# Two parts of a matmul operand moved by 64 and 240 bytes inside their SBUF slot

## The chip, the cores and the metric

The kernel runs on one core of a Trainium2 chip. The metric is device time in microseconds, the median of three runs. All PE (TensorE) work, all vector work on DVE (VectorE), ACT (ScalarE) and POOL (GpSimd), and the transfers issued by SP (SyncE) belong to that one core.

## What is computed

The reference filters each sequence in the frequency domain and then runs a gated feed-forward layer on every token.

```python
def _attn_ref(x, w_r, w_i, b_r, b_i):          # x: 8 x 3008 x 256
    X = np.fft.rfft(x, axis=1)
    Yr = Xr @ w_r - Xi @ w_i + b_r
    Yi = Xr @ w_i + Xi @ w_r + b_i
    # soft threshold by 0.01 on both
    y = np.fft.irfft(Y, n=x.shape[1], axis=1)
def _moe_ref(x, w_in, w_out):                  # x: 24064 x 256, 256 -> 2048 -> 256
    h = x @ w_in
    relu6 = np.clip(h + 3.0, 0.0, 6.0)
    g = h * relu6 / 6.0
    return (g @ w_out).astype(np.float32)
```

## The kernel before

The transform is done as small matmuls (47 by 64 points) with transfers through DRAM between the stages. Those stages are cut into pieces and put between the pieces of the feed-forward layer by a written-out list of slots (`slots`, `fill`).

The feed-forward layer works on 47 blocks of 512 tokens (`c`) and 8 pieces of 256 hidden channels (`f`), which gives 376 units (`units`). Each full-precision matrix product is made of three fp32r products: every operand is split into a high part (the value rounded to fp32r) and a low part (the rest), and low times high, high times low and high times high are added in PSUM.

One unit `i` goes through these steps, which run over four passes of the main loop:

- The input product is done with seven block products of 256 columns (a Strassen scheme; tiles `yb` against `w_in`, into PSUM tiles `pb` and `ps_a`). Each block product is three matmuls: 21 matmuls of 256 columns. ACT and DVE collect them into the tile `h`.
- `gate(i)`: ACT makes `r` from `h` (L1099), DVE makes r = min(r, 6) * h (L1101). ACT then writes the high part of `r` into the tile `gs` in two halves of 512 columns (L1104), and DVE writes the low part, `r` minus high, in one instruction of 1024 columns (L1105).
- `down(i, u, dh)`: four groups, one for each half `u` of the hidden channels and each half `dh` of the output. Each group is three matmuls of 512 columns in this order: `w_out_lo` with high `gs`, `w_out_hi` with high `gs`, `w_out_hi` with low `gs`. That is 12 matmuls of 512 columns for a unit, all through the helper line L137, where `gs` is the moving operand (its columns stream through the array) and `w_out` is the loaded weight. The low part is read by one in three of them: 4 for a unit, 1504 in all.

`gs` has two buffers. A buffer is one slot of 4 * 512 + 64 = 2112 floats for each partition, 64 more than the two parts need; the same slots hold tiles of the first transform (`xin`, `a`, `X`) before the first unit. In the built program both slots start at a multiple of 64 bytes (byte 115840 and byte 124288 of the partition), and so do the buffers of `yb`, of `w_in` and of `w_out`. The order on PE is fixed: what `group`, `phase_1`, `phase_2`, `phase_b` to `phase_e` and `fill` emit stands in program order.

Of the kernel before, what the change touches and what calls it, by code (L numbers as in the profile page):

```python
# [9 lines left out]
F32 = mybir.dt.float32  # L10
F32R = mybir.dt.float32r
# [3 lines left out]
ALU = mybir.AluOpType  # L15
# [6 lines left out]
B, S, D, FF = 8, 3008, 256, 2048  # L22
# [3 lines left out]
P = 128  # L26
# [6 lines left out]
T = 512  # L33
# [68 lines left out]
def spectral_ffn(ctx: ExitStack, tc: tile.TileContext, x, w_r, w_i, bias, w_in, w_out, f47, f64, g64, g64u, sgn, out):  # L102
    nc = tc.nc
# [10 lines left out]
    def space(shape, dt, name, tag=None):  # L114
        tag = tag or name
        return sb.tile(shape, dt, name=name, tag=tag, bufs=depth.get(tag, 1))
# [11 lines left out]
    def split(hi, lo, src, on=None):  # L128

        nc.scalar.copy(out=hi, in_=src)  # L130
        (on or nc.vector).tensor_tensor(out=lo, in0=src, in1=hi.bitcast(F32), op=ALU.subtract)  # L131

    def product(ps, terms, start=True, stop=True, more=False, later=False):

        todo = [p for (ah, al), (bh, bl) in terms for p in (((al, bh), (ah, bh), (ah, bl)) if later else ((al, bh), (ah, bl), (ah, bh)))]
        for n, (a, b) in enumerate(todo):
            nc.tensor.matmul(  # L137
                out=ps,
                lhsT=a,
                rhs=b,  # L140
                start=start and n == 0,
                stop=stop and n == len(todo) - 1,
                skip_group_check=more,
            )
# [26 lines left out]
    wout_s = [const.tile([P, NFT * D], F32R, name="w_out_" + t) for t in ("hi", "lo")]  # L171
# [14 lines left out]
    def behind(g):  # L186

        dep = mybir.DependencyInfo(mybir.DependencyClass.NoSync, mybir.DependencyReason.DATA)
        while True:
            done = len(nc.cur_bb.bb.instructions)  # L190
            last = {}
            for ins in nc.cur_bb.bb.instructions:
                if not type(ins).__name__.startswith("BassTile"):
                    last[ins.engine] = ins
            if next(g, None) is None:
                return
            for ins in nc.cur_bb.bb.instructions[done:]:
                if not type(ins).__name__.startswith("BassTile") and ins.engine in last:
                    tc.add_manual_dep(ins, last[ins.engine].name, dep, reason="order")
            yield  # L200
# [534 lines left out]
    def part(pair, sl):  # L735
        return tuple(t[:, sl] for t in pair)
# [230 lines left out]
    def prepare(c):  # L967
        y = raw.pop(c) if c else raw[c]
        b11, b12, b21, b22 = y[:, 0, :H], y[:, 0, H:], y[:, 1, :H], y[:, 1, H:]
        s = space([P, 4, H], F32, "T")  # L970
        on = nc.gpsimd if c else nc.vector
        sums = [(0, b12, b11), (1, b22, s[:, 0]), (2, b22, b12), (3, b21, s[:, 1])]

        def sum_(n=1):
            for to, p, q in sums[:n]:
                on.tensor_tensor(out=s[:, to], in0=p, in1=q, op=ALU.subtract)
            del sums[:n]

        parts = [(2, b21), (1, b11), (6, s[:, 1]), (7, s[:, 2]), (5, s[:, 0]), (4, s[:, 3]), (3, b22)]
        if c:  # L980
            sum_(4)
        else:
            for n, src in parts[:2]:
                t = space([P, 2, H], F32R, "yb")
                yb[c, n] = (t[:, 0], t[:, 1])
                nc.scalar.copy(out=t[:, 0], in_=src)
                yield
            sum_(2)
            for n, src in parts[:2]:
                hi, lo = yb[c, n]  # L990
                on.tensor_tensor(out=lo, in0=src, in1=hi.bitcast(F32), op=ALU.subtract)
            del parts[:2]
        yield
        for n, src in parts:
            if c == 0:
                sum_({7: 1, 4: 1}.get(n, 0))
            t = space([P, 2, H], F32R, "yb")
            split(t[:, 0], t[:, 1], src, nc.gpsimd if n < 3 else on)
            yb[c, n] = (t[:, 0], t[:, 1])
            yield  # L1000

    units = [(c, f) for c in range(NC) for f in range(nf)]
    hs, ps_of, keep, gs, pos = {}, {}, {}, {}, {}
# [72 lines left out]

    def gate_parts(i):

        at = 0
        t = space([P, 4 * T + 64], F32R, "gs")[:, at : at + 4 * T]  # L1080
        return t.rearrange("p (n u c) -> p n u c", n=2, u=2)

    def gate(i):

        h = hs.pop(i)
        if i == len(units) - 1:
            r = space([P, 2, T], F32, "r")
            t = gs[i] = gate_parts(i)
            for u in (1, 0):
                nc.scalar.activation(out=r[:, u], in_=h[:, u], func=AF.Relu, bias=three, scale=1.0)  # L1090
                nc.vector.scalar_tensor_tensor(
                    out=r[:, u], in0=r[:, u], scalar=6.0, in1=h[:, u], op0=ALU.min, op1=ALU.mult
                )
                split(t[:, 0, u], t[:, 1, u], r[:, u])
            yield
            return
        r = space([P, 2, T], F32, "r")
        for u in range(2):
            nc.scalar.activation(out=r[:, u], in_=h[:, u], func=AF.Relu, bias=three, scale=1.0)  # L1099
        yield  # L1100
        nc.vector.scalar_tensor_tensor(out=r, in0=r, scalar=6.0, in1=h, op0=ALU.min, op1=ALU.mult)  # L1101
        t = gs[i] = gate_parts(i)
        for u in range(2):
            nc.scalar.copy(out=t[:, 0, u], in_=r[:, u])  # L1104
        nc.vector.tensor_tensor(out=t[:, 1], in0=r, in1=t[:, 0].bitcast(F32), op=ALU.subtract)  # L1105
        yield

    def down(i, u, dh):
        c, f = units[i]
        ft = 2 * f + u  # L1110
        ends = i == len(units) - 1
        first, last = f == 0 and u == 0, f == nf - 1 and u == (0 if ends else 1)
        if first:
            pos[dh] = ps_o.tile([P, 512], F32, name=f"po{dh}")
        g = gs[i]
        product(
            pos[dh],
            later=True,
            terms=[(part(wout_s, slice(ft * D + dh * P, ft * D + (dh + 1) * P)), (g[:, 0, u], g[:, 1, u]))],
            start=first,  # L1120
            stop=last,
        )
        if last:
            ot = space([P, T], F32, "ot")
            if ends and dh:
                for n, at in enumerate((slice(0, H), slice(H, T))):
                    if n:
                        nc.vector.tensor_scalar(
                            out=ot[:, at], in0=pos[dh][:, at], scalar1=1.0 / 6.0, scalar2=None, op0=ALU.mult
                        )  # L1130
                    else:
                        nc.scalar.mul(out=ot[:, at], in_=pos[dh][:, at], mul=1.0 / 6.0)
                    nc.sync.dma_start(
                        out=out[dh * P : (dh + 1) * P, c * T + n * H : c * T + (n + 1) * H], in_=ot[:, at]
                    )
                return
            if dh:
                nc.vector.tensor_scalar(out=ot, in0=pos[dh], scalar1=1.0 / 6.0, scalar2=None, op0=ALU.mult)
            else:
                nc.scalar.mul(out=ot, in_=pos[dh], mul=1.0 / 6.0)  # L1140
            nc.sync.dma_start(out=out[dh * P : (dh + 1) * P, c * T : (c + 1) * T], in_=ot)
# [20 lines left out]
    def later():  # L1162

        band()
        stage(EARLY, "exponent")
        stage(EARLY, "clamped")
        band()
        ahead.store()
        last = len(todo_bands) - 1
        for steps in (  # L1170
            ((12, "sums_hi"),),
            ((12, "sums_lo"),),
            ((14, "sign"), (14, "middle")),
            ((14, "rest"), (14, "upper")),
            ((14, "folded"),),
            ((14, "sums_hi"),),
            ((14, "sums_lo"),),
            ((13, "rest"), (13, "upper"), (13, "lower")),
            ((last, "exponent"), (last, "clamped")),
            ((last, "sign"), (last, "middle")),  # L1180
            ((last, "rest"), (last, "upper"), (last, "lower")),
        ):
            yield True
            for n, what in steps:
                stage(n, what)
        yield True
        weights()
        yield True
# [41 lines left out]
    for c in range(1, NC):  # L1230
        g = prepare(c)
# [5 lines left out]
    g = behind(later())  # L1237
    for q in (0, 6, 8, 9, 11, 13, 15, 17, 18, 19, 20, 22, 45):
        slots.setdefault(q, []).append(g)
    g = stage1(1)  # L1240
# [30 lines left out]
    n = len(units)  # L1271
# [4 lines left out]
    def group(i, at):  # L1276
        if 0 <= i < n:
            down(i, *order(i)[at])
# [71 lines left out]
```

## Time and profile before

| what | value |
|---|---|
| median of 3 runs | 2557.91 us (2555.8 to 2558.71) |
| the profiled execution's own time | 2558.67 us |
| its span, first to last instruction | 2556.9 us |
| granted TensorE clock | 1.000 of full speed (2.4 GHz) |
| PE busy | 2536.5 us (99%) |
| weight loads (PEld) busy | 2269.0 us (89%) |
| DVE busy | 1958.9 us (77%) |
| ACT busy | 1953.6 us (76%) |
| POOL busy | 735.2 us (29%) |

The busy time of an engine is the union of its records. PE's matmuls are pipelined: a record of a 256-column matmul lasts 276 ns or more, but the next one starts before it ends, so records overlap and a busy PE says only that the stream has no holes. How fast the stream goes is read from where successive matmuls start.

### The profile page before, as it was taken

The page shows a single profiled execution, that of the slowest core. Times are in us where ns is not written, and L with a number is a line of the kernel's source. Part 1 is how long each engine was busy: PE and PEld are TensorE (multiplying, and loading weights), DVE is VectorE, ACT ScalarE, POOL GpSimd, SP SyncE. Part 2 cuts the span into 40 slices and gives each one's busy share as a digit, 9 for nine tenths or more (in the row PEclk, how much of TensorE's full clock was granted, in tenths as well). Part 3 has the DMA queues.
Part 4 walks back from the last instruction along what each step waited for, and adds up shares of the span by engine and source line. Part 5 has one row for each costly group of instructions (what it writes and reads, how often), then busy time and mean ns, then how long its engine had stood idle before and what let it go on. Part 6 is the DMA issues. An engine that isn't in the chain of part 4 may idle for free.

```text
span 2556.9 us, 45563 instructions
## 1 busy us (share of the span) xinstructions
PE 2536.5 (99%) x16510; PEld 2269.0 (89%) x16510; DVE 1958.9 (77%) x3176; ACT 1953.6 (76%) x4329; POOL 735.2 (29%) x716
## 2 busy tenths in 40 slices
PE   9999999999999999999999999999999999999999
PEld 6788889889999989988899888998989999999998
DVE  6988877777777877777777777777777877777676
ACT  5777777777777777777777777777777777777877
POOL 2223422333133321433313432134311221121210
PEclk9999999999999999999999999999999999999999
DMA  8534422232122321222212322222311121110000
GB/s 279 172 100 136 130 74 72 84 93 75 56 83 80 90 81 53 80 84 81 81 55 78 91 87 67 64 79 82 91 60 60 56 70 53 37 32 25 20 17 17
DMA packets 147321, 199.75 MB, mean 78 GB/s; under 512 B 16319, under 2 KB 102039, under 8 KB 147095
## 3 DMA queue, kind: packets, MB, share of 16 engines
q1 hardware_dynamic: 147095, 196.83, 25.5%
q8 instruction: 130, 2.13, 0.4%
q14 instruction: 96, 0.79, 0.1%
HBM read 99.77 MB, written 74.97 MB: 68 GB/s over the span
## 4 chain that ended last, share of the span: by engine, by line
PE 87%; DVE 4%; ACT 4%; DMA 2%; issue 2%; POOL 0%; SPq 0%; DVEq 0%; ACTq 0%; POOLq 0%
PE po L137 37%; PE ps_a L137 24%; PE pb L137 18%; PE ps_a L871 3%; PE ps_a L757 2%; PE ps_a L472 1%; ACT gs L1104 1%; DVE gs L1105 1%; DVE r L1101 1%; DVE h L1014 1%; ACT r L1099 1%; DMA xin<-in_x 1%; DMA qt<-scr 0%; DVE tc L796 0%; PE ps_a L507 0%
## 5 line engine op out<-in xcount | busy, mean ns | idle before, releaser
L137 PE MATMUL po<-gs,w_out_hi 128*128 128x512 f32 x3008 | 947.6, 395 | 1.0 <-DVE gs L1105 0.8
L1099 ACT ACTIVATE r<-h,three 128x512 f32<-128x512 f32 x750 | 540.8, 724 | 148.7 <-DVE h L1014 133.2
L1101 DVE SCALAR_TENSOR_TENSOR r<-r,h 128x1024 f32<-128x1024 f32 x375 | 491.1, 1309 | 211.0 <-ACT r L1099 210.1
L137 PEld LDWEIGHTS po<-gs,w_out_hi 128*128 128x128 f32 x3008 | 566.2, 188 | 84.8 <-DVE gs L1105 4.7
L137 PE MATMUL po<-gs,w_out_lo 128*128 128x512 f32 x1504 | 610.2, 406 | 0.5 <-ACT ot L1140 0.3
L1105 DVE TENSOR_TENSOR gs<-r,gs 128x1024 fp32r<-128x1024 f32 x375 | 479.5, 1279 | 161.1 <-ACT gs L1104 160.8
L1104 ACT CAST gs<-r 128x512 fp32r<-128x512 f32 x750 | 429.2, 620 | 183.0 <-DVE r L1101 177.5
L137 PE MATMUL pb<-yb,w_in_hi 128*128 128x256 f32 x3004 | 554.0, 278 | 0.0
L137 PEld LDWEIGHTS pb<-yb,w_in_hi 128*128 128x128 f32 x3004 | 458.2, 188 | 34.0
L131 POOL TENSOR_TENSOR yb<-T,yb 128x256 fp32r<-128x256 f32 x184 | 194.9, 1061 | 837.2 <-ACT yb L130 837.2
L137 PE MATMUL ps_a<-yb,w_in_hi 128*128 128x256 f32 x2252 | 428.8, 279 | 0.1
L137 PE MATMUL pb<-yb,w_in_lo 128*128 128x256 f32 x1502 | 422.0, 281 | 3.6 <-ACT u L1011 2.0
L1014 DVE TENSOR_TENSOR h<-ps_a,u 128x256 f32<-128x256 f32 x752 | 313.0, 416 | 116.7 <-PE ps_a L137 113.6
L137 PEld LDWEIGHTS ps_a<-yb,w_in_hi 128*128 128x128 f32 x2252 | 344.0, 188 | 15.9 <-DVE yb L131 0.3
L1011 ACT COPY u<-pb 128x256 f32<-128x256 f32 x752 | 279.1, 372 | 93.3 <-PE pb L137 91.9
L137 PE MATMUL ps_a<-yb,w_in_lo 128*128 128x256 f32 x1126 | 317.2, 282 | 5.1 <-DVE h L1014 4.7
L137 PEld LDWEIGHTS pb<-yb,w_in_lo 128*128 128x128 f32 x1502 | 282.1, 188 | 41.1 <-ACT p L1011 4.2
L137 PEld LDWEIGHTS po<-gs,w_out_lo 128*128 128x128 f32 x1504 | 283.3, 188 | 20.7 <-issue 2.3
L137 PEld LDWEIGHTS ps_a<-yb,w_in_lo 128*128 128x128 f32 x1126 | 211.5, 188 | 30.0 <-DVE h L1014 13.0
L1011 ACT COPY p<-pb 128x256 f32<-128x256 f32 x376 | 138.3, 368 | 32.8 <-PE pb L137 30.5
L1014 DVE TENSOR_TENSOR h<-ps_a,p 128x256 f32<-128x256 f32 x376 | 156.0, 415 | 2.0 <-ACT p L1011 1.4
L1070 ACT COPY h<-pb 128x256 f32<-128x256 f32 x376 | 141.5, 376 | 3.4 <-PE pb L137 3.2
(189 smaller groups left out, 3360.3 us busy)
## 6 DMA issues: line engine op xcount, KB each, us to landing
xin<-in_x SPq DMA_DIRECT2D x48, 512.0 KB, 3.7
bt<-scr SPq DMA_DIRECT2D x96, 256.0 KB, 3.1
scr<-pt SPq DMA_DIRECT2D x96, 256.0 KB, 2.0
out<-ot SPq DMA_DIRECT2D x93, 256.0 KB, 2.0
scr<-a SPq DMA_DIRECT2D x96, 240.0 KB, 2.5
qt<-scr SPq DMA_DIRECT2D x96, 240.0 KB, 3.4
zt<-tc SPq DMA_DIRECT2D x336, 64.0 KB, 2.0
f<-in_f SPq DMA_DIRECT2D x96, 128.0 KB, 2.9
```

The lines of the kernel that those rows point to most:

```text
L131: (on or nc.vector).tensor_tensor(out=lo, in0=src, in1=hi.bitcast(F32), op=ALU.subtract)
L137: nc.tensor.matmul(out=ps, lhsT=a, rhs=b, start=start and n == 0, stop=stop and n == len(todo) - 1, skip_group_check=more,)
L472: nc.tensor.matmul(out=to, lhsT=x[:, xh, dh, which], rhs=w_s[w][wh][:, dh * D : (dh + 1) * D], start=False, stop=n == 2 and (which, dh) == ...
L757: nc.tensor.matmul(out=psv[:, dh, :, u, :], lhsT=data[:, u, dh * P : (dh + 1) * P], rhs=f[:, u, :], start=True, stop=True,)
L871: nc.tensor.matmul(out=ps[:, cs * w + g * rows : cs * w + (g + 1) * rows], lhsT=qt[:rows, cs, g, dh * P : (dh + 1) * P], rhs=f47_s[2][:row ...
L1011: nc.scalar.copy(out=t, in_=ps)
L1014: nc.vector.tensor_tensor(out=hs[i][:, u, half * H : (half + 1) * H], in0=ps, in1=keep.pop((i, n)), op=ALU.add)
L1070: nc.scalar.copy(out=hs[i][:, 1, :H], in_=pb)
L1099: nc.scalar.activation(out=r[:, u], in_=h[:, u], func=AF.Relu, bias=three, scale=1.0)
L1101: nc.vector.scalar_tensor_tensor(out=r, in0=r, scalar=6.0, in1=h, op0=ALU.min, op1=ALU.mult)
L1104: nc.scalar.copy(out=t[:, 0, u], in_=r[:, u])
L1105: nc.vector.tensor_tensor(out=t[:, 1], in0=r, in1=t[:, 0].bitcast(F32), op=ALU.subtract)
```

## The change

`gate_parts` hands out the two parts of a `gs` slot. Before, the high part began at the slot's start and the low part 2 * 512 floats (4096 bytes) behind it. After, the high part begins 16 floats (64 bytes) into the slot, and the low part at float 2 * 512 + 60, which is 240 bytes further than it was. The low part ends at float 2108 of the slot's 2112. The slots themselves, all other tiles, every instruction, their order on each of the five engines and their waits are the same in both programs; only the addresses inside `gs` differ. 64 is a multiple of 64, 32 and 16 bytes; 240 is 3 * 64 + 48, a multiple of 16 bytes and not of 32.

```diff
     def gate_parts(i):
 
-        at = 0
-        t = space([P, 4 * T + 64], F32R, "gs")[:, at : at + 4 * T]
-        return t.rearrange("p (n u c) -> p n u c", n=2, u=2)
+        starts = 16, 2 * T + 60
+        t = space([P, 4 * T + 64], F32R, "gs")
+        return [t[:, at : at + 2 * T].rearrange("p (u c) -> p u c", u=2) for at in starts]
...
         t = gs[i] = gate_parts(i)
         for u in range(2):
-            nc.scalar.copy(out=t[:, 0, u], in_=r[:, u])
-        nc.vector.tensor_tensor(out=t[:, 1], in0=r, in1=t[:, 0].bitcast(F32), op=ALU.subtract)
+            nc.scalar.copy(out=t[0][:, u], in_=r[:, u])
+        nc.vector.tensor_tensor(out=t[1], in0=r, in1=t[0].bitcast(F32), op=ALU.subtract)
         yield
...
-            terms=[(part(wout_s, slice(ft * D + dh * P, ft * D + (dh + 1) * P)), (g[:, 0, u], g[:, 1, u]))],
+            terms=[(part(wout_s, slice(ft * D + dh * P, ft * D + (dh + 1) * P)), (g[0][:, u], g[1][:, u]))],
```

## Rows read from the trace of the kernel before

**Rows 1.** The page's parts 1, 2 and 4: busy time, clock by slice, the chain.

```profile
PE 2536.5 (99%) x16510; PEld 2269.0 (89%) x16510; DVE 1958.9 (77%) x3176; ACT 1953.6 (76%) x4329; POOL 735.2 (29%) x716
...
PEclk9999999999999999999999999999999999999999
...
PE 87%; DVE 4%; ACT 4%; DMA 2%; issue 2%; POOL 0%; SPq 0%; DVEq 0%; ACTq 0%; POOLq 0%
```

**Rows 2.** Waits of PE, then of its weight loads: us in total, times, longest.

```profile
PE ps_a L137 <- DVE h L1014: 5.6, 12, 0.9
PE pb L137 <- ACT u L1011: 2.0, 5, 0.9
...
PE po L137 <- DVE gs L1105: 0.8, 2, 0.4
...
PEld ps_a L137 <- DVE h L1014: 14.1, 25, 1.2
...
PEld po L137 <- DVE gs L1105: 4.7, 12, 0.8
```

**Rows 3.** Groups of PE by line: names, shapes, count, busy us, mean ns, idle before.

```profile
L137 PE MATMUL po<-gs,w_out_hi 128*128 128x512 f32 x3008 | 947.6, 395 | 1.0 <-DVE gs L1105 0.8
L137 PE MATMUL pb<-yb,w_in_hi 128*128 128x256 f32 x3004 | 554.0, 278 | 0.0
L137 PE MATMUL ps_a<-yb,w_in_hi 128*128 128x256 f32 x2252 | 428.8, 279 | 0.1
```

**Rows 4.** Instructions on the tile gs: count, ns min/median/max, first and last start.

```profile
L137 PE MATMUL po<-gs,w_out_hi x3008: 388/394/506, 113.4 to 2553.0; 128*128 128x512 f32 x188
...
L137 PE MATMUL po<-gs,w_out_lo x1504: 388/393/801, 113.0 to 2552.6; 128*128 128x512 f32 x188
...
L1105 DVE TENSOR_TENSOR gs<-r,gs x375: 1207/1226/2378, 113.5 to 2547.2; 128x1024 fp32r<-128x1024 f32 x188
```

**Rows 5.** Timeline of one unit, PE, DVE and ACT: start us, us, instruction.

```profile
2346.80 0.39 PE L137 MATMUL po<-gs,w_out_lo 128*128 128x512 f32 x1
...
2347.84 0.28 PE L137 MATMUL pb<-yb,w_in_lo 128*128 128x256 f32 x1
...
2348.18 0.28 PE L137 MATMUL ps_a<-yb,w_in_lo 128*128 128x256 f32 x1
...
2348.52 0.39 PE L137 MATMUL po<-gs,w_out_lo 128*128 128x512 f32 x1
...
2349.21 0.40 PE L137 MATMUL po<-gs,w_out_lo 128*128 128x512 f32 x1
...
2349.36 1.14 ACT L1104 CAST gs<-r 128x512 fp32r<-128x512 f32 x2 [0.61 <-DVE r L1101]
...
2350.54 1.22 DVE L1105 TENSOR_TENSOR gs<-r,gs 128x1024 fp32r<-128x1024 f32 x1 [0.54 <-ACT gs L1104]
...
2351.29 0.28 PE L137 MATMUL ps_a<-yb,w_in_lo 128*128 128x256 f32 x1
...
2351.64 0.28 PE L137 MATMUL ps_a<-yb,w_in_lo 128*128 128x256 f32 x1
...
2352.00 0.39 PE L137 MATMUL po<-gs,w_out_lo 128*128 128x512 f32 x1
```

**Rows 6.** Groups of PE at 2348.00:2348.45, then at 2351.50:2351.75 of that unit.

```profile
L137 PE MATMUL pb<-yb,w_in_hi 128*128 128x256 f32 x2 | 0.4, 276 | 0.0
...
L137 PE MATMUL ps_a<-yb,w_in_lo 128*128 128x256 f32 x2 | 0.6, 281 | 0.0
```

**Rows 7.** Groups at 2347.43:2347.48 and 2349.16:2349.20: the low-part matmul alone.

```profile
L137 PE MATMUL po<-gs,w_out_hi 128*128 128x512 f32 x1 | 0.4, 398 | 0.0
...
L137 PE MATMUL po<-gs,w_out_hi 128*128 128x512 f32 x1 | 0.4, 393 | 0.0
```

**Rows 8.** Stretches of one unit each: us, busy us (count) by engine, clock, DMA.

```profile
2352.00:2357.20 5.20, 5.20 (x36) 4.68 (x35) 3.54 (x6) 4.02 (x8) 0.00 (x0) 1.00 0.00 0
2357.20:2362.40 5.20, 5.20 (x36) 4.68 (x35) 3.54 (x6) 4.02 (x8) 0.00 (x0) 1.00 0.00 0
...
379.65:384.88 5.23, 5.23 (x35) 4.71 (x34) 4.15 (x7) 4.38 (x9) 0.00 (x0) 1.00 0.01 3
...
692.97:698.20 5.23, 5.23 (x35) 4.71 (x34) 4.15 (x7) 4.38 (x9) 0.00 (x0) 1.00 0.01 3
```

More of the change, by code (lines that the diff above doesn't have):

```diff
@@ L1093, in gate @@
                 )
-                split(t[:, 0, u], t[:, 1, u], r[:, u])
+                split(t[0][:, u], t[1][:, u], r[:, u])
             yield
```

## Prediction

> **What bounds the kernel now.** I read the page's shares and its chain first. PE is busy for 2536.5 of 2556.9 us and holds 87% of the chain, at the full granted clock in every slice, 2.4 GHz [rows 1]. Then the waits: the longest entry of PE is 5.6 us in total and that of its weight loads 14.1 us, and waits for the low part of `gs` come to 0.8 and 4.7 us [rows 2]. The reader is to see that PE has no holes worth speaking of. The time of this kernel is therefore the sum of the steps from one matmul's start to the next one's.
>
> So the next view is the timeline, which shows how long such a step is. In one unit near the end, three matmuls of 256 columns take from 2347.84 to 2348.18, 0.34 us, and three others, with the same shapes and the same kind of operands, take from 2351.29 to 2351.64, 0.35 us [rows 5]. The records of the first kind last 276 ns and of the second 281 ns [rows 6]. Nothing waits in either place; the difference is a different step, 4 to 5 ns of some 115. A record's length follows its step, so I use it as the finer measure of a step. The matmuls of 512 columns spread in the same way: at least 388 ns, median 394 [rows 4]. Their step is 0.23 us: the group from 2348.52 to 2349.21 has three of them [rows 5]. The low-part matmul, the third of each group, lasts 398 ns behind the first group of this unit and 393 ns behind the second, and the other two groups repeat 398 and 393 [rows 7].
>
> Does another engine cause the long step? Two stretches of one unit each, without any transform work, take 5.20 us near the end, and two earlier ones of the same 33 matmuls take 5.23 us [rows 8]. In all four POOL does nothing and DMA next to nothing. A whole unit can thus run at two paces, 0.03 us or 0.6% apart, with PE full in both. The pace depends on how successive streams through PE meet, and it is carried on from one matmul to the next. That is what a change of address can touch here, and nothing else in this kernel is near the path.
>
> **What the change removes, adds and moves.** No instruction is added, removed or moved; no wait changes. Three things get other addresses.
>
> First, ACT's two writes of the high part (L1104) and DVE's write of the low part (L1105). I cost both at nothing. In the unit shown L1105 starts at 2350.54 and takes 1.22 us, so it ends at 2351.76; the group that reads it starts at 2352.00, and its third matmul, the first to read the low part, comes two steps of 0.23 us later, at 2352.46 [rows 5]. The cover is 0.70 us. Were it used up, each further ns of L1105 would cost PE 1 ns in 375 units, 0.4 us in all; but L1105 would have to go from 1226 to about 1930 ns first [rows 4]. A gain there would be worth nothing either, for the same reason.
>
> Second, PE's reads of the high part, 3008 matmuls with one start of 64 bytes further. The old start was at a multiple of 64 bytes and the new one is too. Wherever operands in this program lie, they begin at such a multiple as far as these products go, and both paces occur among them. I see nothing that a further move of the same kind would change, and take zero, with the bounds below.
>
> Third, PE's reads of the low part, 1504 matmuls. This is the only stream in the fp32r products that will begin off a 64-byte boundary, 48 bytes past one. No row of before shows such a stream, so the cost is bounded from both sides.
>
> - From below: each low-part matmul drops to the shortest record of its group. The group `w_out_hi`, half of which reads the low part, has a mean of 395 ns [rows 3] and a minimum of 388 [rows 4]. That is 7 ns x 1504 = 10.5 us gained.
> - From above: each rises to the long record of this unit, 398 ns [rows 7]: 3 ns x 1504 = 4.5 us lost.
> - The matmuls that follow can be carried along. The 256-column ones lie between 276 and 281 ns [rows 6], with means of 278 (3004 of them) and 279 (2252) in the two groups that hardly wait [rows 3]. All at 276 would give 2 x 3004 + 3 x 2252 ns = 12.8 us; all at 281 would cost 3 x 3004 + 2 x 2252 ns = 13.5 us.
>
> Together the bounds are 23.3 us down and 18.0 us up.
>
> **Which value I take.** The low-part matmuls now stand nearer the long end than the short end: 398 and 393 ns against 388. What sets the step is how a stream meets its neighbours, so a stream that starts elsewhere within its 64 bytes should meet them differently, and there is more room below than above, 7 ns to 3. I take the full 7 ns, because the paces are few and held, not a spread around a mean: a stream that leaves the long pace goes to the short one. For the 256-column matmuls both directions are open by nearly the same amount, and I take zero. Sum: -10.5 us. Against the profiled execution's 2558.67 us that is 2548.2; that execution stands 0.76 us above the median of the three runs, so for the median it is 2557.91 - 10.5 = 2547.4 us. This is a choice between bounds, not a measured price.
>
> **The rivals.**
>
> Rival 1, nothing changes: a start 48 bytes past a boundary is as good as any other, or the paces only swap places and average out over 376 units. For it speaks that the trace holds both paces throughout with every fp32r operand starting at a multiple of 64 bytes, so alignment alone doesn't choose between them. Against it speaks that a unit falls into one of two repeated patterns (5.20 or 5.23 us), which is the behaviour of something with a fixed phase, not of noise. Time: 2557.9 us, within 0.2% (5.1 us), which is about what a measurement of this kernel can tell from no change.
>
> The Trainium skill bears on this rival. Its page "SBUF — State Buffer", section "Specifications (TRN2)", says that SBUF has 16-byte cachelines and that an access pays for each crossing to a new line. Both new starts are multiples of 16 bytes, so by that rule not one line more is touched and the time would stay at 2557.9. The same page, section "Who interferes with whom", has PE waiting on no other engine's access; the trace agrees in so far as the long step appears with POOL and DMA at rest, but it says nothing on why one and the same matmul has two steps.
>
> Rival 2, slower: each low-part read now touches 33 pieces of 64 bytes where it touched 32, since it starts 48 bytes into the first. If PE takes its moving operand by such pieces and every piece costs its share of the step, one more costs 0.23 us / 32 = 7.2 ns [rows 5], an estimate from that row. Times 1504 this is 10.8 us: 2568.7 us. It decides as soon as the mean of the `w_out_hi` group rises by half of that, to about 398.6 ns, with the 256-column groups unchanged. For it: 64 bytes is what 16 columns hold, and the unaligned start is the one thing in this change that no stream had before. Against it: no row shows that a piece is charged separately. The swing of the 256-column matmuls to their long pace, up to 13.5 us, would look the same from outside and ends at a similar time, 2571.4.
>
> Rival 3, a part of the gain and a swing of the followers to the short pace: the low bound, 2557.9 - 23.3 = 2534.6 us. For it: in the unit shown the groups of 256 columns at 2347.84 are already short and those at 2351.29 long [rows 5, 6], so the long ones could join. Against it: the unit time of 5.20 us is repeated unchanged by the units around it [rows 8], so the long ones are as firmly held as the short ones.
>
> **How the numbers follow.** A gain of about 10 us from the low-part matmuls: 0.37. Rival 3, a gain of 15 us or more: 0.08. Rival 1: 0.25. Rival 2 in either form: 0.30. So faster by over 0.2% has 0.45, the same 0.25, slower 0.30. The likeliest gives 2547 us. Its own range is 2539 to 2553. Since cases of both signs hold much of the chance, the range for 8 times in 10 runs from 2537 (most of rival 3 left out) to 2570 (rival 2 within, the full swing of the followers left out).
>
> **What would show it in the profile of the changed kernel.** The group `w_out_hi` should have a mean of about 391 to 392 ns in place of 395, since one half of it falls to 388, and the low-part matmul of a late unit, read alone, 388 and not 398. `w_out_lo` and the waits should stand as they were. A unit without transform work should take about 5.17 us, four times 7 ns less than 5.20. L1105 should keep its median of 1226 ns. The prediction is wrong if the `w_out_hi` mean stays at 395 with the same two unit times (rival 1), if it rises to 398 or more (rival 2), or if the main move is in the `pb` and `ps_a` groups of 256 columns, whose paces I have left where they are; it is wrong in its ground if L1105 grows so long that PE's waits for it rise from 5.5 us to more than a few tens.

## The result, and the profile after

The changed kernel takes 2576.15 us, the median of four runs (2575.78 to 2576.64), beside 2558.31 us for the kernel before (four runs, 2555.80 to 2559.15). The ratio is 1.0076, with a 95% interval of 1.0064 to 1.0088: slower by 17.8 us. The prediction said 2547 us with a range up to 2570, so it missed in sign and the time lies outside the range.

The profiled execution took 2576.31 us, with a span of 2574.5 us, 17.6 us more than before. Its page gives these busy times, clock slices and shares of the chain:

```profile
PE 2556.6 (99%) x16510; PEld 2282.7 (89%) x16510; DVE 1957.2 (76%) x3176; ACT 1965.0 (76%) x4329; POOL 734.1 (29%) x716
...
PEclk9999999999999999999999999999999999999999
...
PE 91%; DVE 4%; ACT 2%; issue 1%; DMA 1%; POOL 0%; SPq 0%; DVEq 0%; ACTq 0%; POOLq 0%
```

PE is busy for 20.1 us more than in [rows 1], with the same 16510 matmuls at the same clock. The next view is the waits of PE, then of its weight loads (us in total, times, longest):

```profile
PE ps_a L137 <- DVE h L1014: 4.2, 11, 0.7
PE pb L137 <- ACT u L1011: 1.7, 4, 0.8
...
PE po L137 <- DVE gs L1105: 0.8, 2, 0.4
...
PEld ps_a L137 <- DVE h L1014: 11.6, 21, 1.2
...
PEld po L137 <- DVE gs L1105: 4.3, 10, 0.8
```

None of them is longer than in [rows 2], and PE's idle time as a whole (the span less the busy time) falls from 20.4 to 17.9 us. A slower PE waits less for the others. So no new wait explains the loss, and it must lie in the steps of the stream. The groups of PE by line, as in [rows 3]:

```profile
L137 PE MATMUL po<-gs,w_out_hi 128*128 128x512 f32 x3008 | 951.2, 397 | 1.0 <-DVE gs L1105 0.8
...
L137 PE MATMUL po<-gs,w_out_lo 128*128 128x512 f32 x1504 | 616.0, 410 | 0.2 <-ACT gs L1104 0.2
...
L137 PE MATMUL pb<-yb,w_in_hi 128*128 128x256 f32 x3004 | 562.9, 280 | 0.0
...
L137 PE MATMUL ps_a<-yb,w_in_hi 128*128 128x256 f32 x2252 | 429.5, 280 | 0.0
```

`w_out_hi` went from 395 to 397 ns, `pb` from 278 to 280, `ps_a` from 279 to 280. The `w_out_lo` group, of which [rows 3] show nothing, had a mean of 406 ns before and has 410 now. The change moves no operand of the `pb` and `ps_a` groups, and they are slower too.

The three instructions on the tile `gs`, as in [rows 4] (ns min/median/max):

```profile
L137 PE MATMUL po<-gs,w_out_hi x3008: 387/397/502, 113.2 to 2570.7; 128*128 128x512 f32 x188
...
L137 PE MATMUL po<-gs,w_out_lo x1504: 388/401/801, 112.9 to 2570.2; 128*128 128x512 f32 x188
...
L1105 DVE TENSOR_TENSOR gs<-r,gs x375: 1209/1226/2330, 113.3 to 2564.9; 128x1024 fp32r<-128x1024 f32 x188
```

DVE's write has the same median as before. The `w_out_lo` matmul, which reads only the high part, went from a median of 393 to 401 ns, the largest move among the groups of the unit. A stretch of one unit without transform work, in the columns of [rows 8], takes 5.29 us where it took 5.20 or 5.23:

```profile
2366.53:2371.82 5.29, 5.29 (x35) 4.73 (x34) 3.54 (x6) 4.05 (x8) 0.00 (x0) 1.00 0.00 0
```

It is not a single case. The trace holds 91 stretches from one unit's first `w_out_lo` matmul to the next unit's that have the 33 matmuls alone. Before, 59 of them take 5.200 us and 14 take 5.233 or 5.234; after, 49 take 5.293 or 5.294 and 27 take 5.285 or 5.286.

Where do the 0.09 us above the commoner pace of before lie? These are the groups of PE in that one stretch:

```profile
L137 PE MATMUL po<-gs,w_out_hi 128*128 128x512 f32 x8 | 2.5, 397 | 0.0
L137 PE MATMUL po<-gs,w_out_lo 128*128 128x512 f32 x4 | 1.6, 399 | 0.0
...
L137 PE MATMUL pb<-yb,w_in_hi 128*128 128x256 f32 x8 | 1.5, 280 | 0.0
```

And these are the same groups in a unit of the kernel before, the first stretch of [rows 8]:

```profile
L137 PE MATMUL po<-gs,w_out_hi 128*128 128x512 f32 x8 | 2.5, 395 | 0.0
L137 PE MATMUL po<-gs,w_out_lo 128*128 128x512 f32 x5 | 2.0, 392 | 0.0
...
L137 PE MATMUL pb<-yb,w_in_hi 128*128 128x256 f32 x8 | 1.5, 276 | 0.0
```

With 8, 4 and 8 such matmuls in a unit, the difference is 8 x 2 + 4 x 7 + 8 x 4 = 76 ns, most of the 90. The rest is spread over the other groups, which rose by 1 or 2 ns each. The loss is a change of pace of the whole stream. By their order in the trace, the `w_out_hi` matmuls that read the high part can be told from those that read the low part, the ones I had looked at: the mean of the first goes from 395.0 to 395.2 ns, that of the second from 395.7 to 398.4. Summed from each start to the next over the whole kernel, the low-part matmuls lose 4.0 us, the `w_out_lo` matmuls 5.5, the 256-column matmuls of the units 5.6 and those of the transform 2.4, of 17.6 us in all.

### The profile page after: what moved, and what is told of

Read it like the earlier page. It is cut to its first block, busy times and chain, and to the rows that moved or that the text cites. A ratio compares the mean times of both kernels' runs of the same rounds, so it can differ in the third digit from the quotient of the medians.

```text
span 2574.5 us, 45563 instructions
## 1 busy us (share of the span) xinstructions
PE 2556.6 (99%) x16510; PEld 2282.7 (89%) x16510; DVE 1957.2 (76%) x3176; ACT 1965.0 (76%) x4329; POOL 734.1 (29%) x716
## 4 chain that ended last, share of the span: by engine, by line
PE 91%; DVE 4%; ACT 2%; issue 1%; DMA 1%; POOL 0%; SPq 0%; DVEq 0%; ACTq 0%; POOLq 0%
PE po L137 38%; PE ps_a L137 25%; PE pb L137 19%; PE ps_a L871 3%; PE ps_a L757 3%; PE ps_a L472 1%; DVE r L1101 1%; ACT gs L1104 1%; DVE gs L1105 1%; DVE h L1014 0%; PE ps_a L507 0%; ACT r L1099 0%; PE pb L438 0%; DMA xin<-in_x 0%; DVE tc L796 0%
## 5 line engine op out<-in xcount | busy, mean ns | idle before, releaser
L1105 DVE TENSOR_TENSOR gs<-r,gs 128x1024 fp32r<-128x1024 f32 x375 | 478.9, 1277 | 163.0 <-ACT gs L1104 162.6
L137 PE MATMUL pb<-yb,w_in_hi 128*128 128x256 f32 x3004 | 562.9, 280 | 0.0
```

The costliest lines, as they stand in the source:

```text
L137: nc.tensor.matmul(out=ps, lhsT=a, rhs=b, start=start and n == 0, stop=stop and n == len(todo) - 1, skip_group_check=more,)
L1105: nc.vector.tensor_tensor(out=t[1], in0=r, in1=t[0].bitcast(F32), op=ALU.subtract)
```

## The experiments

In all of them the instructions, their order and their waits in the kernel are those of the change; only addresses inside the `gs` slot differ, unless said. "High" and "low" below are how many bytes the part's start lies behind where it was in the kernel before. The kernel before is thus 0 and 0, and the change is 64 and 240. Each edit is given against the change's `starts = 16, 2 * T + 60`.

**Low part alone: 0 and 240.**

```diff
-        starts = 16, 2 * T + 60
+        starts = 0, 2 * T + 60
```

> High part back at the slot's start, low part 240 bytes further as in the change. Theory A (the start of PE's read of the low part, 48 bytes past a multiple of 64, sets the pace of the stream): the whole loss, about 2576 us, mean of the w_out_hi group about 397 ns. Rival B (the high part's 64 bytes matter): 2558 us. Rival C (it is the distance between the two parts, 4272 bytes against 4096): about 2576 us here too, so this run does not part A from C.

Measured: 2543.56 us (five runs) beside 2556.91, ratio 0.9949 (0.9937 to 0.9962). It is faster than before by 13.4 us, and faster than the change by 32.6 us, though it differs from the change only by 64 bytes in the high part. The low part's odd start by itself is therefore not what costs. None of the three theories had this run faster than before. Its groups:

```profile
L137 PE MATMUL po<-gs,w_out_hi 128*128 128x512 f32 x3008 | 947.8, 395 | 1.0 <-DVE gs L1105 0.9
...
L137 PE MATMUL po<-gs,w_out_lo 128*128 128x512 f32 x1504 | 607.3, 404 | 0.9 <-ACT ot L1140 0.7 <-ACT gs L1104 0.2
...
L137 PE MATMUL pb<-yb,w_in_hi 128*128 128x256 f32 x3004 | 551.1, 277 | 0.0
...
L137 PE MATMUL ps_a<-yb,w_in_hi 128*128 128x256 f32 x2252 | 423.3, 277 | 0.0
```

The group that holds the moved matmul stands at 395 as before: by their order in the trace, its low-part matmuls fell by 1.8 ns and its high-part ones rose by 1.3. Most of the gain is in its followers, at 277 in place of 278 and 279.

**Both parts by 64: 64 and 64.**

```diff
-        starts = 16, 2 * T + 60
+        starts = 16, 2 * T + 16
```

> Both parts 64 bytes further, low part again 4096 bytes behind the high one and at a multiple of 64. Theory A: no loss, 2558 us. Rival B (the high part's 64 bytes): 2576 us, or a good part of it. Rival C (distance): 2558 us.

Measured: 2557.21 us (eleven runs) beside 2556.91, ratio 1.0001 (0.9992 to 1.0010). A move of the high part by 64 bytes is not what costs either, where the low part moves along. The time is the same, but the groups are not:

```profile
L137 PE MATMUL po<-gs,w_out_hi 128*128 128x512 f32 x3008 | 936.1, 392 | 1.0 <-DVE gs L1105 0.9
...
L137 PE MATMUL pb<-yb,w_in_hi 128*128 128x256 f32 x3004 | 564.2, 280 | 0.0
```

`w_out_hi` has fallen to 392, the very sign by which I wanted to know a gain of 10 us, and the followers have risen from 278 to 280 and taken it back.

**Low part by 16: 0 and 16.**

```diff
-        starts = 16, 2 * T + 60
+        starts = 0, 2 * T + 4
```

> High part at the slot's start, low part only 16 bytes further than before. Theory A in its form that any start off a multiple of 64 bytes costs the same: about 2576 us. Theory A in its form that the phase within 64 bytes counts: any time within some 20 us of 2558, but not 2558 itself. If only starts off a multiple of 16 bytes cost something: 2558 us.

Measured: 2558.21 us (eleven runs) beside 2556.91, ratio 1.0005 (0.9996 to 1.0013): the same. A start off a 64-byte boundary neither costs nor gains by itself.

**Written as before, read 16 bytes earlier.** The parts are written at 0 and 0. PE reads the low part from 16 bytes ahead of where it begins, which is 240 modulo 256, so its columns are displaced by four.

```diff
-        starts = 16, 2 * T + 60
+        starts = 0, 2 * T
...
-        return [t[:, at : at + 2 * T].rearrange("p (u c) -> p u c", u=2) for at in starts]
+        return [t[:, at : at + 2 * T].rearrange("p (u c) -> p u c", u=2) for at in (*starts, 2 * T - 4)]
...
-            terms=[(part(wout_s, slice(ft * D + dh * P, ft * D + (dh + 1) * P)), (g[0][:, u], g[1][:, u]))],
+            terms=[(part(wout_s, slice(ft * D + dh * P, ft * D + (dh + 1) * P)), (g[0][:, u], g[2][:, u]))],
```

> Both parts are written where they were before the change; PE alone reads the low part from 16 bytes ahead of it, that is 48 bytes past a multiple of 64 as in the change, and the writes of ACT and DVE keep their old addresses. The low operand is thereby shifted by four columns, so this run's output is not the reference's. Theory A (PE's read): about 2576 us. Rival D (the addresses that DVE writes to): 2558 us.

Measured: 2543.59 us (five runs) beside 2556.91, ratio 0.9950 (0.9938 to 0.9963). That is the first experiment's time to 0.03 us; neither forecast, 2576 or 2558, came true. Where ACT and DVE write plays no part; only where PE reads does. It also says that 16 bytes earlier and 240 bytes later are the same start to PE.

**PE alone, all starts.** The 33 matmuls of a unit in the kernel's order, on operands at the kernel's places, with no other engine's work between them: four high starts (0, 64, 128, 192) by sixteen low starts (0 to 240 in steps of 16), six units of each, once forwards and once backwards. It computes nothing of the reference.

```python
COMBOS = [(h, l) for h in (0, 16, 32, 48) for l in range(0, 64, 4)]
COMBOS += COMBOS[::-1]
...
        hi, lo = (t[:, s : s + 2 * T].rearrange("p (u c) -> p u c", u=2) for s in (h, 2 * T + 64 + l))
        units(hi, lo, COUNT)
```

> The matmuls of one unit alone: PE repeats the 33 matmuls of a unit in the kernel's order, with no transform, no gate, no transfers in between, six units for each of 64 pairs of starts (high part at 0, 64, 128, 192 bytes, low part at 0 to 240 bytes in steps of 16 behind an even place), then the same pairs backwards. Its output is not the reference's. Theory A2 (the step between two matmuls hangs on where the second stream starts relative to the one before it): the unit time is the same for all pairs with the same difference low minus high, and takes several values from about 5.10 to 5.31 us; difference 0 gives about 5.20, 240 less than 5.20, 176 more. Rival B2 (each part's own place within 256 bytes counts): pairs with one difference disagree. Rival E (other engines are needed for it): all 64 pairs within 0.2% of one another.

Measured (one run, 4111.48 us in all): one unit takes from 5.15 to 5.41 us, by the pair of starts alone. These are stretches of one unit each, in the columns of [rows 8], for the pairs 0/0, 0/16, 0/48, 0/176, 0/192, 0/240, 64/48, 64/64, 64/160, 64/240, 192/176, and 0/0 again at the end of the second pass:

```profile
46.85:52.05 5.20, 5.20 (x36) 4.68 (x35) 0.00 (x0) 0.00 (x0) 0.00 (x0) 1.00 0.00 0
78.15:83.37 5.22, 5.22 (x36) 4.69 (x35) 0.00 (x0) 0.00 (x0) 0.00 (x0) 1.00 0.00 0
140.93:146.08 5.15, 5.15 (x36) 4.63 (x35) 0.00 (x0) 0.00 (x0) 0.00 (x0) 1.00 0.01 3
391.65:396.85 5.20, 5.20 (x36) 4.66 (x35) 0.00 (x0) 0.00 (x0) 0.00 (x0) 1.00 0.00 0
422.73:427.88 5.15, 5.15 (x36) 4.63 (x35) 0.00 (x0) 0.00 (x0) 0.00 (x0) 1.00 0.00 0
516.37:521.53 5.16, 5.16 (x36) 4.64 (x35) 0.00 (x0) 0.00 (x0) 0.00 (x0) 1.00 0.00 0
641.47:646.69 5.22, 5.22 (x36) 4.73 (x34) 0.00 (x0) 0.00 (x0) 0.00 (x0) 1.00 0.00 0
672.71:677.90 5.19, 5.19 (x35) 4.72 (x34) 0.00 (x0) 0.00 (x0) 0.00 (x0) 1.00 0.00 0
860.69:865.87 5.18, 5.18 (x35) 4.66 (x34) 0.00 (x0) 0.00 (x0) 0.00 (x0) 1.00 0.00 0
1016.84:1022.13 5.29, 5.29 (x35) 4.73 (x34) 0.00 (x0) 0.00 (x0) 0.00 (x0) 1.00 0.00 0
1895.90:1901.30 5.40, 5.40 (x35) 4.75 (x34) 0.00 (x0) 0.00 (x0) 0.00 (x0) 1.00 0.00 0
4028.44:4033.67 5.23, 5.23 (x36) 4.71 (x35) 0.00 (x0) 0.00 (x0) 0.00 (x0) 1.00 0.00 0
```

DVE, ACT and POOL do nothing, and PE is full. The pair 0/0 gives 5.20 us in one pass and 5.23 in the other, the two paces of [rows 8]; 64/240 gives the 5.29 of the change. So PE needs no other engine to fall into these paces. What matters is the pair: taken alone, the low part's 240 is faster (5.16), and so is 64 for the high part with the low part left at 0 (5.193 us, from start to start of its units); the two together are the slow 5.29. The difference of the two starts does not settle it: 0/240 and 64/48 are both 16 bytes short of 256 apart and give 5.16 and 5.22.

**Low read 16 ahead of a high at 64: 64 and 48.** This keeps the distance of the two parts' starts that the first experiment has (16 bytes short of 256), at another place.

```diff
-        starts = 16, 2 * T + 60
+        starts = 16, 2 * T + 16
...
-        return [t[:, at : at + 2 * T].rearrange("p (u c) -> p u c", u=2) for at in starts]
+        return [t[:, at : at + 2 * T].rearrange("p (u c) -> p u c", u=2) for at in (*starts, 2 * T + 12)]
...
-            terms=[(part(wout_s, slice(ft * D + dh * P, ft * D + (dh + 1) * P)), (g[0][:, u], g[1][:, u]))],
+            terms=[(part(wout_s, slice(ft * D + dh * P, ft * D + (dh + 1) * P)), (g[0][:, u], g[2][:, u]))],
```

> Both parts written 64 bytes further, the low part read by PE from 16 bytes ahead of where it lies: the difference low minus high is 240 (that is, -16) modulo 256 as in the two faster runs, but the high part starts 64 bytes on as in the change. The low operand is shifted by four columns, so the output is not the reference's. Theory A2 (the difference counts): about 2544 us. Rival B2 (the places count, and 64 for the high part with an odd low part is the slow pair): slower than 2558, near 2576 us.

Measured: 2562.09 us (eleven runs) beside 2557.39, ratio 1.0017 (1.0008 to 1.0026). A theory by which the distance of the two parts decides wanted 2544 here. The rival, slower than 2558 and near 2576, has its sign right and not its size.

**The change's distance at another place: 0 and 176.**

```diff
-        starts = 16, 2 * T + 60
+        starts = 0, 2 * T + 44
```

> High part at the slot's start, low part 176 bytes further: the difference of the change (176 modulo 256) without its 64 bytes for the high part. Theory A2: about 2576 us. Rival B2 (a high part at the start is what made the two runs faster, and 48 bytes past a multiple of 64 is what counts for the low one): about 2544 us.

Measured: 2557.07 us (eleven runs) beside 2557.39, ratio 0.9999 (0.9990 to 1.0008). The change has the same distance of 176 and takes 2576.15. With this run the theory of the distance falls; each part's own place counts. The simple rule of places in the rival, which wanted 2544, falls too.

**The best of the map: 0 and 48.**

```diff
-        starts = 16, 2 * T + 60
+        starts = 0, 2 * T + 12
```

> High part at the slot's start, low part 48 bytes further. The run of PE alone has its shortest unit here, 5.153 us against 5.200 or 5.233 for the starts of before, 5.167 for low 240 alone (2543.6 us in the kernel) and 5.293 for the change (2576 us). Theory I (the kernel follows the unit time of PE alone, about 0.7 of 376 units' difference): faster than the run with low 240 alone, about 2541 us. Rival J (in the kernel the transform pieces between the units break the pattern, so that the unit time of PE alone tells little): anything from 2544 to 2576.

Measured: 2543.72 us (five runs) beside 2557.36, ratio 0.9946 (0.9933 to 0.9958). PE alone had named it among the shortest units, and in the kernel it is as fast as the first experiment.

**A multiple of 64 in the low part: 0 and 192.**

```diff
-        starts = 16, 2 * T + 60
+        starts = 0, 2 * T + 48
```

> High part at the slot's start, low part 192 bytes further: both at a multiple of 64 bytes. PE alone has 5.153 us for it too. Theory I: about 2541 us. What the prediction assumed (a move by a multiple of 64 bytes changes nothing): 2557 us.

Measured: 2545.23 us (five runs) beside 2557.36, ratio 0.9951 (0.9937 to 0.9965). All starts are multiples of 64 bytes here, as in the kernel before, and the time is 12 us less.

**The worst of the map: 192, low read at 176.**

```diff
-        starts = 16, 2 * T + 60
+        starts = 48, 2 * T + 48
...
-        return [t[:, at : at + 2 * T].rearrange("p (u c) -> p u c", u=2) for at in starts]
+        return [t[:, at : at + 2 * T].rearrange("p (u c) -> p u c", u=2) for at in (*starts, 2 * T + 44)]
...
-            terms=[(part(wout_s, slice(ft * D + dh * P, ft * D + (dh + 1) * P)), (g[0][:, u], g[1][:, u]))],
+            terms=[(part(wout_s, slice(ft * D + dh * P, ft * D + (dh + 1) * P)), (g[0][:, u], g[2][:, u]))],
```

> High part 192 bytes further, low part written 192 bytes further and read by PE from 16 bytes ahead of it (176 modulo 256): the longest unit of PE alone, 5.407 us. The low operand is shifted by four columns, so the output is not the reference's. Theory I: about 2605 us, 1.9% above before. Rival J: within 20 us of 2557.

Measured: 2594.66 us (four runs) beside 2557.36, ratio 1.0145 (1.0132 to 1.0159). In this kernel the low-part matmuls themselves lose most: by their order in the trace their mean goes from 395.7 to 413.3 ns. A unit of this kernel without transform work takes what PE alone took:

```profile
2380.70:2386.11 5.41, 5.41 (x35) 4.76 (x34) 3.55 (x6) 4.04 (x8) 0.00 (x0) 1.00 0.00 0
```

That holds beyond this kernel. In the kernel before, the change and all ten variants of it, the commonest time of a unit without transform work, from start to start, is the time of PE alone for that pair to 1 ns: 5.200 us before, 5.293 in the change, from 5.153 (0/48 and 0/192) to 5.407 in the others.

**A pair in the middle: 64 and 160.**

```diff
-        starts = 16, 2 * T + 60
+        starts = 16, 2 * T + 40
```

> High part 64 bytes further as in the change, low part 160 bytes further in place of 240. PE alone has a unit of 5.180 us here against 5.293 for the change. Eight starts so far give a line through the kernel's time of about 0.2 us for each ns of the unit time of PE alone, from 2543.7 us at 5.153. Theory I (the pair of starts decides, as PE alone shows it): about 2549 us, faster than before, although the high part stands where the change puts it. Rival K (with a high part 64 bytes on, any low start other than the same 64 loses): 2562 us or more.

Measured: 2550.28 us (seven runs) beside 2557.84, ratio 0.9971 (0.9960 to 0.9982). With the high part at 64, as in the change, 80 bytes less in the low part's start are worth 25.9 us. Of the four forecasts made from PE alone, 2541, 2541, 2605 and 2549 us for 0/48, 0/192, 192/176 and this pair, all have the right sign, and the first three are 3 to 10 us too far out.

**Like matmuls in a row.** 24 matmuls of one shape at a time, with nothing of the reference in them: 256 or 512 columns, the moving operand at 0 to 240 bytes in steps of 16, the weights at 0, 64, 128, 192 or 16 bytes (modulo 256), and 64 in place of 128 weight columns as a last set.

```python
    for size, cols, w_at in CASES:
        for m_at in range(0, 64, 4):
            for n in range(COUNT):
                a = w[:, w_at + 512 * (n % 2) : w_at + 512 * (n % 2) + cols]
                b = m[:, m_at + 512 * (n % 2) : m_at + 512 * (n % 2) + size]
                nc.tensor.matmul(out=po[n % 2][:cols, :size], lhsT=a, rhs=b, start=True, stop=True)
```

> PE alone: 24 like matmuls in a row, with 256 or 512 columns, the moving operand starting at 16 places 16 bytes apart, the weights at five places (0, 64, 128, 192 and 16 bytes further), and once with half as many weight columns (64 for 128). Its output is not the reference's. Theory F (what costs is PE's two reads of SBUF, columns and next weights, meeting each other): the step changes with the moving operand's place, as a function of the difference of the two places, and with 64 weight columns it is shorter and changes less. Rival G (the moving stream alone, its own pieces, sets the step): the step hangs on the moving operand's place alone, and is the same with 64 weight columns. Rival H (only the jump from one start to the next counts): no dependence at all here, since the start is kept over the 24.

Measured (one run, 906.68 us in all). Four stretches of 24 matmuls of 256 columns each, for the (weight, moving) starts 0/112, 64/112, 64/176 and 16/128:

```profile
52.55:55.27 2.72, 2.72 (x26) 2.72 (x25) 0.00 (x0) 0.00 (x0) 0.00 (x0) 1.00 0.00 0
97.67:100.51 2.84, 2.84 (x26) 2.84 (x25) 0.00 (x0) 0.00 (x0) 0.00 (x0) 1.00 0.00 0
109.10:111.82 2.72, 2.72 (x26) 2.72 (x25) 0.00 (x0) 0.00 (x0) 0.00 (x0) 1.00 0.00 0
236.55:239.43 2.88, 2.88 (x26) 2.88 (x25) 0.00 (x0) 0.00 (x0) 0.00 (x0) 1.00 0.02 6
```

The first and second differ only in where the weights lie: 113 ns become 118 ns for a matmul (2.72 and 2.84 us over 24). The third moves the streamed operand by the same 64 bytes as the weights, and the short step is back. So neither the moving stream alone (rival G) nor the jump from one start to the next (rival H) sets the step. The list of sixteen steps repeats, shifted by four places, for weights moved by 64, 128 and 192 bytes: over both widths, 88 of 93 places agree to 0.3 ns, and the other five are off by up to 2.2. For weights moved by 16 bytes it does not: the fourth stretch keeps the difference of 112 and takes 120 ns. So the places of PE's two reads matter together; for weights that lie multiples of 64 bytes apart, as all in this kernel do, the difference of the two starts gives the step of nearly all like matmuls, and otherwise more than the difference counts.

Is it the length of the weight read? With 64 weight columns, these are two stretches of 256 columns (moving starts 144 and 240):

```profile
729.65:732.37 2.72, 2.72 (x26) 2.72 (x25) 0.00 (x0) 0.00 (x0) 0.00 (x0) 1.00 0.00 0
746.42:749.30 2.88, 2.88 (x26) 2.88 (x25) 0.00 (x0) 0.00 (x0) 0.00 (x0) 1.00 0.00 0
```

The step still runs from 113 to 120 ns, so a shorter weight read does not remove the effect. It does change it: the shortest steps are at other places, and at 512 columns the steps run from 226.7 to 232.2 ns (mean 229.5) with 64 weight columns, and to 234.6 (mean 231.9) with 128. These are 24 matmuls of 512 columns at the moving start 208, with 128 and then with 64 weight columns:

```profile
331.85:337.48 5.63, 5.63 (x25) 4.52 (x24) 0.00 (x0) 0.00 (x0) 0.00 (x0) 1.00 0.01 3
821.03:826.47 5.44, 5.44 (x25) 3.22 (x24) 0.00 (x0) 0.00 (x0) 0.00 (x0) 1.00 0.01 3
```

Theory F, two reads that meet, wanted a shorter step that changes less with half the weight columns. At 512 columns it came out so, at 256 hardly. The theory is neither refuted nor shown.

The kernels beside the unit of PE alone (the stretches above):

| high, low read | unit of PE alone, us | kernel, us | ratio to before |
|---|---|---|---|
| 0, 48 | 5.15 | 2543.72 | 0.9946 |
| 0, 192 | 5.15 | 2545.23 | 0.9951 |
| 0, 240 | 5.16 | 2543.56 and 2543.59 | 0.9949, 0.9950 |
| 64, 160 | 5.18 | 2550.28 | 0.9971 |
| 64, 64 | 5.19 | 2557.21 | 1.0001 |
| 0, 176 | 5.20 | 2557.07 | 0.9999 |
| 0, 0 (before) | 5.20 and 5.23 | 2556.91 to 2558.31 | 1 |
| 0, 16 | 5.22 | 2558.21 | 1.0005 |
| 64, 48 | 5.22 | 2562.09 | 1.0017 |
| 64, 240 (the change) | 5.29 | 2576.15 | 1.0076 |
| 192, 176 | 5.40 | 2594.66 | 1.0145 |

From the first to the last row the kernel grows by 50.9 us and the unit by 0.25 us, so 1 ns of the unit is worth 0.2 us of the kernel. All 376 units would give 0.376 us. About half of that arrives. The traces show where it goes missing: in the 91 stretches of the 33 matmuls alone, the last row is 235 ns longer than the first on average, nearly all of the bench's 254; in the 284 that hold transform matmuls as well, it is 102 ns. That these matmuls break the pattern up fits, but no run took them out of the kernel. The ranking is rough: 64/64 lies some 5 us above a straight line between the ends, no faster than 0/176.

## Why the prediction was wrong

**What held.** PE's stream sets the time, and what an address can touch is its pace: every run agrees. The writes by ACT and DVE at nothing: L1105 keeps its median of 1226 ns, and the kernel that writes as before and reads elsewhere has the time of the one that writes there too. PE's idle time did not grow.

**The step that failed** is the second one, "I see nothing that a further move of the same kind would change, and take zero", for the 64 bytes of the high part. With the low part at 240, they cost 32.6 us (2576.15 against 2543.56). Of the 3008 matmuls of that step, `w_out_lo` alone loses 5.5 us. I had taken the size of the boundary (multiples of 64) as what counts. What counts is the place modulo 256 bytes, by the map and by the run that reads 16 bytes earlier; the kernel with the low part at 192, all of whose starts are multiples of 64, is 12 us faster than before. The rows could have warned me: both paces occurred with every start at a multiple of 64, which I used only to say that alignment does not choose between them.

**The form of the sum was wrong as well.** I priced the two parts apart and added. Two moves that each leave PE alone at or below its old pace (64/0 at 5.193, 0/240 at 5.16) make it slower together (5.29). No sum over parts can give that.

**The third step, the low-part matmul at -10.5 us, failed too.** In the change its mean rises from 395.7 to 398.4 ns, which is 2.7 ns x 1504 = 4.1 us lost, close to the upper bound of 4.5. The ground for the choice, that a stream which leaves the long pace goes to the short one, does not hold: before, the four low-part matmuls of a unit last 398 and 393 ns in turn, and in the unit of the change shown above all four last 399. That the low part moved alone gains 13.4 us, near the 10.5, is luck: there these matmuls fall by 1.8 ns and not by 7, the `w_out_hi` mean stays at 395, and the followers fall. The term that I set to zero, the followers, carries most of the gain there, 8.0 of the 17.6 us lost in the change, and the balance at 64/64, where 392 in `w_out_hi` is paid back by 280 in `pb`.

**The rivals.** Rival 2's first form, a price for the 33rd piece of 64 bytes, is refuted: 0/16 and 0/240 both read such a piece, and are the same and faster. Its second form, the swing of the followers to the long pace, is a part of what happened: 8.0 us by the sums above. The `w_out_lo` matmul, which no rival of mine moved, and the low-part matmul went along. I gave that form up to 13.5 us; 17.8 were measured in all. Rival 1's rule from the Trainium skill ("SBUF — State Buffer", section "Specifications (TRN2)": accesses pay for the 16-byte cachelines that they cross) would leave all these kernels at one time, since every start is a multiple of 16 bytes. The measurement decides: they run from 2543.56 to 2594.66 us. The Trainium skill's page "TensorE: Matmul & The Clock Gate", section "Step-by-step: what each phase is for", says that "Loading the next tile's weights doesn't steal SBUF read bandwidth from the running matmul." The row of like matmuls speaks against that as a rule without limits: its step goes from 113 to 118 ns when only the weights move by 64 bytes. No run shows that it is read bandwidth that is lost.

**What is shown and what stays open.** Shown: the pace hangs on where PE's streamed operands start modulo 256 bytes, in the rows of like matmuls also on where the weights start, and PE alone reproduces it: to 1 ns in units without transform work, roughly in the whole kernel. The starts do not fix it alone, since 0/0 has two paces. Argued only: that the two reads get in each other's way inside SBUF; a dependence on the places of both speaks for it, and so do the shorter steps at 512 columns with half the weight columns, but no run looked inside. Open: why a given pair is good or bad. The difference of starts explains nearly all like matmuls; the kernel's mixture of 256- and 512-column matmuls it does not, and I have no formula that gives 5.15 or 5.40 from the starts.

## What to carry to other kernels

When PE is full at the top clock and one matmul shows more than one step, the start addresses of the streamed operands, modulo 256 bytes, are a parameter worth about 2% (2543.6 to 2594.7 us here; weights were moved only in the rows of like matmuls), and it is found by trying pairs, not by rounding to a boundary. A bench of PE alone with the kernel's own order of matmuls ranks the pairs well enough to pick from: a low part 48 bytes further with the high part where it was gives 0.9946 of the time before. Do not price such a move by the matmul that it touches, since the gain or loss may stand in the matmuls behind it.

## What was not expected of the hardware

- The step of a 256-column fp32r matmul at 2.4 GHz, in a row of like ones with nothing else running, is 113 to 120 ns (2.72 to 2.88 us for 24) by the operands' places, with the weights at multiples of 64 bytes.
- Half the weight columns leave that range as it is, the same 2.72 and 2.88 us, but put the shortest steps at other places; at 512 columns they shorten the mean step from 231.9 to 229.5 ns.
- The pace of a unit is held to the nanosecond, and nearly always comes in grains: from start to start, the pairs of the table give 5.153, 5.167, 5.180, 5.193, 5.200, 5.207, 5.220, 5.233, 5.293 and 5.407 us, each within 1 ns of a multiple of 6.667 ns, which is 16 periods of the 2.4 GHz clock. Three of the map's 64 pairs do otherwise: 64/112 holds 5.250 us, half a grain off, and 64/176 and 128/16 alternate between two times.
- One pair (0/0) has two stable paces, 5.20 and 5.23 us, with no other engine at work. In the map it takes the one in the first pass and the other in the second, so what ran before it may decide; no run tested that.
